# One share-split load per round, and a shorter VectorE chain per attention head, in a two-round cached decode kernel

## The chip, the cores and the metric

The kernel runs on one core of one Trainium2 chip. The metric is the device time of one execution in microseconds (us). Before the change it is 713.51 us, the median of three executions (712.98, 713.51, 714.87).

## What is computed

One token for each of 4 sequences goes twice through an attention layer and a two-matrix layer. Both rounds use the same weights and the same cache; of the cache only the last 1024 positions are read.

```
x = A_x                                        # (4, 1, 640)
for _ in range(2):
    q = layernorm(x) @ wq                      # 32 heads of 128
    scores = einsum("bhqd,bhkd->bhqk", q, k_cache[:, :, -1024:]) * 128 ** -0.5
    x = x + einsum("bhqk,bhkd->bhqd", softmax(scores), v_cache[:, :, -1024:]) @ wo
    x = x + maximum(layernorm(x) @ w1, 0) @ w2 # 640 -> 1728 -> 640
```

All numbers are float32. Each round reads every head's query weights, keys, values and output weights, and both matrices of the second layer, so about 302 MB cross from HBM to the core in one execution. The weights are read twice because the on-chip memory holds only a part of them.

## The kernel before

**Tiling.** The host lays everything that belongs to one head out as a *record*: 128 rows (partitions) of 9472 columns, in the order query weights (`WQ`, 640 columns), keys (`K`, 4096), values (`V`, 4096) and output weights (`WO`, 640). The tensor `rec` has the 32 records side by side. The tensor `wm` holds the two matrices of the second layer. On the chip the tile `store` has five slots of one record each; `ring`, `kept` and `kept2` hold further pieces.

**Loads.** A list `items` of pieces is made ahead, in the order in which they are needed; `piece`, `run` and `group` append to it. `pump` issues as many of them as have free room, from SyncE (SP). When an engine has used a piece, `done` marks its columns free and calls `pump` again, so a load's place in SP's program follows the work that frees its room, and SP waits there for that work. Before the change each load takes all 128 rows of a range of columns.

**Work of a head.** The loop over heads is written so that the work of neighbouring heads overlaps. TensorE (PE) runs its instructions in program order. For step n it computes the scores of head n+1 (`scores`, into one of two PSUM tiles `sc_ps`), the values product of head n (`values`, into `o_ps`), the query of head n+2 (`query`, into `misc`), and then the transposed output and the projection of head n (`output_T` into `o_ps`, `project` into `acc`). VectorE (DVE) finds the maximum of the scores, which ScalarE (ACT) needs for the exponentials (`softmax`); then VectorE transposes the exponentials in blocks of 32, scales them by one over their sum (`weights`) and picks the four diagonal blocks out of the values product (`picks`). The first records of round 2 are partly loaded while the second layer of round 1 runs. `park` and `unpark` hold some columns in PSUM meanwhile, and `mlp` is the second layer. `busy` issues matmuls whose results are not used.

**Lines.** Every instruction after the first few is recorded by the helper `InOrder`, so the profile gives nearly all of them line 104 (L104) and they are told apart by the names of their tiles: `sc_ps<-store,qT` are the scores, `o_ps<-store,scratch` the values product, `misc<-xT,store` the query, `o_ps<-pick,scratch` the transposed output, and `acc<-store,oTs` the projection. `acc<-store,scratch` is the last product of the second layer, and `store<-rec`, `ring<-wm` and `store<-wm` are loads. `t_ps<-sc_ps` is the transpose in `weights`, and `scratch<-o_ps,of_block` is `picks`.

## Time and profile before

| | |
|---|---|
| median of three executions | 713.51 us |
| the profiled execution's own time | 713.65 us |
| its span (first to last instruction) | 711.9 us |
| what lies around the span | 1.75 us |
| bytes read from HBM | 301.87 MB |
| PE, DVE, ACT busy | 498.0, 355.4, 95.9 us |
| mean granted TensorE clock | 0.83 |

The profile is of one execution. "Span" runs from the first to the last instruction. A row of a group names the engine, the operation, the tile written and the tiles read, the shape, how often it occurs, the busy time in us, the mean duration in ns, and after the second bar the idle time just before it with what ended that. A row by stretches of time gives, for each engine, the busy time and in brackets the number of instructions, then the granted clock, the mean busy share of the 16 DMA engines and the GB/s they moved. SPq is SP's queue of load issues.

### The profile page before, as it was taken

What the parts mean: (1) busy time and instruction counts of PE and PEld (TensorE: products, weight loads), DVE (VectorE), ACT (ScalarE), POOL (GpSimd) and SP (SyncE); (2) the same over time, 40 slices, a digit from 0 to 9 for tenths busy, and PEclk for the clock granted to TensorE, in tenths of its full rate; (3) what the DMA queues carried; (4) which work ended last, traced back from release to release, by engine and by line L of the source; (5) the groups of instructions that cost most, each with busy time, mean ns of one, the idle gap of its engine ahead of it and who ended that gap; (6) DMA issues with size and microseconds to landing.
All of it is one profiled execution on the core that took longest, in us unless ns stands there. A gap on an engine that the chain in (4) does not pass through costs nothing.

```text
span 711.9 us, 8953 instructions
## 1 busy us (share of the span) xinstructions
PE 498.0 (70%) x3718; PEld 200.7 (28%) x3718; DVE 355.4 (50%) x1008; ACT 95.9 (13%) x152; POOL 1.1 (0%) x9
## 2 busy tenths in 40 slices
PE   4387396476675576868878899666584578686976
PEld 2122132232321233333213343232231232233322
DVE  3254265253463354546741887644272454473761
ACT  1111010011010110111120321101010011020111
POOL 0000000000000000000000000000000000000000
PEclk9987678678787777788999999867697777788899
DMA  9999999999999999999999999999999999999996
GB/s 410 408 450 410 452 417 449 416 446 442 420 428 450 427 427 419 436 433 427 426 403 393 420 433 429 445 430 439 434 448 418 430 445 428 428 419 431 428 427 277
DMA packets 14760, 302.52 MB, mean 425 GB/s; under 512 B 1648, under 2 KB 2304, under 8 KB 6784
## 3 DMA queue, kind: packets, MB, share of 16 engines
q1 hardware_dynamic: 14688, 301.95, 99.0%
q8 instruction: 29, 0.48, 0.2%
q14 instruction: 11, 0.09, 0.0%
q10 hardware_dynamic: 32, 0.01, 0.0%
HBM read 301.87 MB, written 0.08 MB: 424 GB/s over the span
## 4 chain that ended last, share of the span: by engine, by line
DMA 75%; PE 20%; DVE 4%; issue 1%; ACT 0%; SPq 0%; DVEq 0%
DMA store<-rec 69%; PE o_ps L104 7%; PE sc_ps L104 6%; PE misc L104 4%; DMA ring<-wm 3%; DMA store<-wm 3%; PE acc L104 3%; DVE scratch L104 2%; DVE oTs L104 1%; DVE small L104 0%; ACT sc_ps L104 0%; PE t_ps L104 0%; SPq L104 0%; DVE store L104 0%; DVE t_ps L104 0%
## 5 line engine op out<-in xcount | busy, mean ns | idle before, releaser
L104 PE MATMUL sc_ps<-store,qT 128*4 128x512 f32 x1014 | 185.9, 827 | 33.4 <-DMA store<-rec 31.5
L104 PE MATMUL misc<-xT,store 128*128 128x4 f32 x640 | 99.0, 281 | 124.4 <-DMA store<-rec 124.0
L104 ACT ACTIVATE sc_ps<-sc_ps,small 128x1024 f32<-128x1024 f32 (+1 forms) x68 | 76.7, 1127 | 535.8 <-DVE small L104 535.3
L104 PEld LDWEIGHTS misc<-xT,store 128*128 128x128 f32 x640 | 93.4, 227 | 182.7 <-DMA store<-rec 150.9
L104 PE MATMUL o_ps<-store,scratch 128*16 128x512 f32 x956 | 140.3, 665 | 2.7 <-DVE scratch L104 1.5
L104 DVE TENSOR_REDUCE small<-sc_ps 128x1 f32<-128x1024 f32 x64 | 78.1, 1221 | 93.3 <-PE sc_ps L104 93.3
L104 DVE STREAM_TRANSPOSE t_ps<-sc_ps 128x512 f32<-128x512 f32 x128 | 93.1, 728 | 2.1
L104 DVE COPY qT<-misc 128x4 f32<-128x4 f32 x64 | 10.0, 156 | 142.8 <-PE misc L104 142.8
L104 DVE SCALAR_TENSOR_TENSOR scratch<-o_ps,of_block,scratch 128x128 f32<-128x128 f32 x186 | 65.2, 350 | 6.6
L104 PEld LDWEIGHTS sc_ps<-store,qT 128*4 128x4 f32 x1014 | 32.3, 106 | 113.6 <-issue 65.5
L104 PEld LDWEIGHTS o_ps<-store,scratch 128*16 128x16 f32 x956 | 32.1, 111 | 111.7 <-issue 67.6
L104 PE MATMUL acc<-store,oTs 128*4 128x160 f32 x478 | 33.4, 359 | 14.6 <-DVE oTs L104 13.2
L104 DVE TENSOR_SCALAR scratch<-o_ps,of_block 128x128 f32<-128x128 f32 x62 | 21.7, 350 | 30.4 <-PE o_ps L104 30.4
L104 PE MATMUL o_ps<-pick,scratch 128*128 128x4 f32 x124 | 26.6, 285 | 13.8 <-DVE scratch L104 13.8
L104 DVE TENSOR_TENSOR scratch<-t_ps,mrt 128x64 f32<-128x64 f32 x128 | 28.7, 225 | 4.7
L104 PEld LDWEIGHTS o_ps<-pick,scratch 128*128 128x128 f32 x124 | 22.5, 226 | 21.4 <-DVE scratch L104 18.8
L104 PE MATMUL misc<-store,small 128*1 128x512 f32 (+1 forms) x40 | 18.6, 570 | 1.7 <-DMA store<-rec 1.7
L104 DVE COPY oTs<-o_ps 128x4 f32<-128x4 f32 x58 | 9.4, 161 | 19.1 <-PE o_ps L104 18.6
L104 DVE TENSOR_SCALAR mrt<-of_batch,small 128x4 f32<-128x4 f32 x64 | 14.7, 230 | 2.2
L104 DVE STREAM_TRANSPOSE scratch<-small 128x32 f32<-128x32 f32 x64 | 12.9, 202 | 1.1 <-ACT sc_ps L104 1.1
L104 PEld LDWEIGHTS acc<-store,oTs 128*4 128x4 f32 x478 | 6.7, 84 | 20.6 <-DVE oTs L104 17.7
L104 ACT ACTIVATION_READ_ACCUMULATOR sc_ps<-sc_ps,small 128x1 f32 x64 | 12.2, 191 | 0.0
(76 smaller groups left out, 118.1 us busy)
## 6 DMA issues: line engine op xcount, KB each, us to landing
store<-rec SPq DMA_DIRECT2D x10, 7872.0 KB, 25.8
store<-rec SPq DMA_DIRECT2D x5, 7936.0 KB, 32.3
store<-rec SPq DMA_DIRECT2D x15, 2368.0 KB, 20.1
store<-rec SPq DMA_DIRECT2D x6, 4736.0 KB, 26.2
store<-rec SPq DMA_DIRECT2D x4, 6336.0 KB, 27.7
store<-rec SPq DMA_DIRECT2D x2, 7104.0 KB, 28.8
store<-rec SPq DMA_DIRECT2D x2, 6272.0 KB, 43.6
store<-rec SPq DMA_DIRECT2D x2, 4416.0 KB
```

What stands on the lines that cost most here:

```text
L104: r = build(*args, **kwargs)
```

## The change

Three things change.

1. **Loads.** In each round one record (head 25 in round 1, head 8 in round 2) gets its first 512 columns by a load of its own. The host stores these 512 columns a second time in a new tensor `shares` of 16 rows, 8 for each round. A row holds what 16 partitions of the tile take, one partition after the other (16 times 512 numbers), and 32 numbers of padding. The load's source is therefore 8 shares of 16 rows, where all other loads have 128 rows. The rest of the record comes as before, 8960 columns wide. The bytes moved are the same.
2. **VectorE.** `picks` is one product over 512 columns, written back into PSUM, and one sum over the four blocks, in the place of four instructions over 128 columns. `weights` transposes all 1024 columns in place and scales them in one instruction, in the place of two transposes into `t_ps` and two scalings.
3. **ScalarE.** It takes over four small operations per head: the copies to `qT` and to `oTs`, the product `nmax * rstd` in `softmax`, and `mrt` in `weights`. With the reading of the accumulated sum, which it did before, these are five small instructions beside the exponentials.

```
+SHARE = 512
+SHARED = [25, 8]
...
+    def shared(r, h):
+        src = shares[8 * r:8 * r + 8, :16 * SHARE].rearrange("g (p c) -> g p c", c=SHARE)
+        items.append((src, "store", home(h, r) * REC, SHARE, [(("rec", r, h), 0, SHARE, home(h, r) * REC)]))
+
     def piece(r, h, lo, hi, buf="store", col=None):
+        if h == SHARED[r]:
+            shared(r, h)
+            lo = SHARE
         run(r, h * REC + lo, h * REC + hi, buf, home(h, r) * REC + lo if col is None else col)
...
-        dve.tensor_copy(qT, misc[:, 8:8 + B])
+        act.copy(qT, misc[:, 8:8 + B])
...
-        dve.tensor_tensor(nmax, nmax, rstd, op=OP.mult)
+        act.activation(nmax, nmax, AF.Copy, scale=rstd)
         act.activation(sc_ps[s], sc_ps[s], AF.Exp, bias=nmax, scale=rstd, accum_out=tot[s])
 
-    def weights(s, parts=(0, 1)):
-        if 0 in parts:
+    def weights(s, parts=((0, 2),)):
+        if parts[0][0] == 0:
 
             dve.transpose(spread, tot[s].to_broadcast([P, 32]))
             dve.reciprocal(rtot, spread[:, 0:1])
-            dve.tensor_scalar(mrt, of_batch, rtot, None, op0=OP.mult)
-        for i in parts:
-            dve.transpose(t_ps, sc_ps[s][:, 512 * i:512 * i + 512])
-            dve.tensor_tensor(wT[:, i], t_ps.rearrange("p (c j) -> p c j", j=32)[:, :, :B],
-                              mrt.unsqueeze(1).to_broadcast([P, 16, B]), op=OP.mult)
+            act.activation(mrt, of_batch, AF.Copy, scale=rtot)
+        for i, j in parts:
+            w = sc_ps[s][:, 512 * i:512 * j]
+            dve.transpose(w, w)
+            dve.tensor_tensor(wT[:, i:j].rearrange("p i c j -> p (i c) j"),
+                              w.rearrange("p (c j) -> p c j", j=32)[:, :, :B],
+                              mrt.unsqueeze(1).to_broadcast([P, 16 * (j - i), B]), op=OP.mult)
...
     def picks(last):
-        o, on_ = outs[last], on[last]
-        dve.tensor_scalar(on_, o[:, :DH], of_block[:, 0:1], None, op0=OP.mult)
-        for c in range(1, 4):
-            dve.scalar_tensor_tensor(on_, o[:, DH * c:DH * c + DH], of_block[:, c:c + 1], on_, op0=OP.mult, op1=OP.add)
-
-    def output_T(i, last=False, by_act=False):
+        o = outs[last].rearrange("p (c d) -> p c d", c=4)
+        dve.tensor_tensor(o, o, of_block.unsqueeze(2).to_broadcast([P, 4, DH]), op=OP.mult)
+        dve.tensor_reduce(on[last], o.rearrange("p c d -> p d c"), op=OP.add, axis=AX.X)
+
+    def output_T(i, last=False):
         pe.matmul(outs[last][:, :B], on[last], pick, start=True, stop=True)
-        if by_act:
-            act.copy(oTs[:, i], outs[last][:, :B])
-        else:
-            dve.tensor_copy(oTs[:, i], outs[last][:, :B])
+        act.copy(oTs[:, i], outs[last][:, :B])
...
+        "shares": np.pad(np.concatenate([rec[h, :, :SHARE].reshape(8, 16 * SHARE) for h in SHARED]), ((0, 0), (0, 32))),
```

The last heads of a round keep two halves of 512 columns in `weights`, as before (`((0, 1),)`, `((1, 2),)` and `((0, 1), (1, 2))`). The added lines move the helper's line from 104 to 106.

The first place is SP, at the load of record 25 in round 1. `store<-rec 128x9472` is one whole record, and the wider loads ahead of it hold several records or parts of them. Before:

```order
L104 DMA store<-rec 128x15872
L104 DMA store<-rec 128x15744
L104 DMA store<-rec 128x9472
L104 DMA store<-rec 128x7296
L104 DMA kept<-rec 128x1536
```

With the change:

```order
L106 DMA store<-rec 128x15872
L106 DMA store<-rec 128x15744
L106 DMA store<-shares 128x1x512
L106 DMA store<-rec 128x8960
L106 DMA store<-rec 128x7296
L106 DMA kept<-rec 128x1536
```

The record's first 512 columns became a load of their own ahead of the rest; nothing else in SP's order moved.

The second place is VectorE, at the picks and weights of one early head in round 1, up to the next head's maximum (`sc_ps_74` and `sc_ps_75` are the two score tiles). Before:

```order
L104 TENSOR_SCALAR scratch<-o_ps,of_block 128x128
L104 SCALAR_TENSOR_TENSOR scratch<-o_ps,of_block,scratch 128x128 x3
L104 COPY qT<-misc 128x4
L104 COPY oTs<-o_ps 128x4
L104 STREAM_TRANSPOSE scratch<-small 128x32
L104 RECIPROCAL small<-scratch 128x1
L104 TENSOR_SCALAR mrt<-of_batch,small 128x4
L104 STREAM_TRANSPOSE t_ps<-sc_ps_75 128x512
L104 TENSOR_TENSOR scratch<-t_ps,mrt 128x64
L104 STREAM_TRANSPOSE t_ps<-sc_ps_75 128x512
L104 TENSOR_TENSOR scratch<-t_ps,mrt 128x64
L104 TENSOR_REDUCE small<-sc_ps_74 128x1
```

With the change:

```order
L106 TENSOR_TENSOR o_ps<-o_ps,of_block 128x512
L106 TENSOR_REDUCE scratch<-o_ps 128x128
L106 STREAM_TRANSPOSE scratch<-small 128x32
L106 RECIPROCAL small<-scratch 128x1
L106 STREAM_TRANSPOSE sc_ps_75<-sc_ps_75 128x1024
L106 TENSOR_TENSOR scratch<-sc_ps_75,mrt 128x128
L106 TENSOR_REDUCE small<-sc_ps_74 128x1
```

Fourteen instructions became seven; the fifteenth, the product `nmax * rstd` that follows the maximum, went as well.

The third place is ScalarE, in the early heads of round 1. Before, it has one instruction per head in this list (the reading of the sum belongs to it):

```order
L104 ACTIVATE sc_ps_74,small<-sc_ps_74,small 128x1024
L104 ACTIVATE sc_ps_75,small<-sc_ps_75,small 128x1024
L104 ACTIVATE sc_ps_74,small<-sc_ps_74,small 128x1024
L104 ACTIVATE sc_ps_75,small<-sc_ps_75,small 128x1024
L104 ACTIVATE sc_ps_74,small<-sc_ps_74,small 128x1024
```

With the change one head has:

```order
L106 COPY qT<-misc 128x4
L106 COPY oTs<-o_ps 128x4
L106 ACTIVATE mrt<-of_batch,small 128x4
L106 ACTIVATE small<-small 128x1
L106 ACTIVATE sc_ps_74,small<-sc_ps_74,small 128x1024
```

The two copies, `mrt` and the product for the maximum now stand between two exponentials in ScalarE's order.

More of the change, by code (lines that the diff above doesn't have):

```diff
@@ L111, in decode_kernel @@
 @with_exitstack
-def decode_kernel(ctx: ExitStack, tc: tile.TileContext, xf, rec, wm, out):
+def decode_kernel(ctx: ExitStack, tc: tile.TileContext, xf, rec, shares, wm, out):
     nc = tc.nc
@@ L517, in decode_kernel @@
                 scores(r, hs[-1], 1)
-                weights(s, (0,))
+                weights(s, ((0, 1),))
             if r and n < NS - 2:
                 busy(256, sc_ps[n % 2], 2, H - 1)
-            output_T(max(i, 0), by_act=end)
+            output_T(max(i, 0))
             if i < 0:
@@ L526, in decode_kernel @@
         softmax(1)
-        weights(0, (1,))
+        weights(0, ((1, 2),))
         values(r, hs[-2], 0, (0, 1))
-        weights(1)
+        weights(1, ((0, 1), (1, 2)))
         picks(0)
@@ L533, in decode_kernel @@
             park(0)
-        output_T(late - 2, by_act=True)
+        output_T(late - 2)
         if not r:
```

## Prediction

> **What bounds the kernel now.** I read the page's table of load queues first, then the chain of work that ended last, then the last microseconds in half-microsecond stretches. The page:
>
> ```profile
> span 711.9 us, 8953 instructions
> ...
> DMA packets 14760, 302.52 MB, mean 425 GB/s; under 512 B 1648, under 2 KB 2304, under 8 KB 6784
> ...
> q1 hardware_dynamic: 14688, 301.95, 99.0%
> q8 instruction: 29, 0.48, 0.2%
> q14 instruction: 11, 0.09, 0.0%
> q10 hardware_dynamic: 32, 0.01, 0.0%
> ...
> DMA 75%; PE 20%; DVE 4%; issue 1%; ACT 0%; SPq 0%; DVEq 0%
> ```
>
> The loads (q1) take 99.0% of what 16 DMA engines have in the span, and DMA holds 75% of the last chain. Two stretches show that this is so throughout, and two more show the change of rounds:
>
> ```profile
> 40.00:340.00 300.00, 203.21 (x1426) 82.78 (x1429) 147.74 (x414) 34.98 (x54) 0.00 (x0) 0.78 1.00 431
> ...
> 400.00:680.00 280.00, 204.93 (x1517) 83.39 (x1517) 155.29 (x437) 38.25 (x60) 0.00 (x0) 0.80 1.00 432
> ...
> 367.00:375.00 8.00, 5.77 (x43) 1.08 (x36) 0.48 (x3) 0.29 (x1) 0.00 (x0) 1.00 0.99 375
> 375.00:387.00 12.00, 10.44 (x137) 3.91 (x132) 0.87 (x2) 1.08 (x3) 0.00 (x0) 1.00 0.99 386
> ```
>
> In the 580 us of the first two rows the DMA share is 1.00, at 431 and 432 GB/s, while VectorE is busy about half the time. No VectorE time is saved there unless it lets a load start that otherwise would not; the engines have no free time in which it could run. What can still move the end is how evenly the 16 engines finish:
>
> ```profile
> 703.00:704.00 1.00, 1.00 (x36) 0.74 (x24) 0.00 (x0) 0.00 (x0) 0.00 (x0) 1.00 0.96 399
> 704.00:704.50 0.50, 0.25 (x4) 0.00 (x0) 0.00 (x0) 0.00 (x0) 0.00 (x0) 1.00 0.65 266
> 704.50:705.00 0.50, 0.00 (x0) 0.00 (x0) 0.00 (x0) 0.00 (x0) 0.00 (x0) 1.00 0.53 220
> 705.00:705.50 0.50, 0.00 (x0) 0.00 (x0) 0.00 (x0) 0.00 (x0) 0.00 (x0) 1.00 0.51 210
> 705.50:706.00 0.50, 0.00 (x0) 0.00 (x0) 0.00 (x0) 0.00 (x0) 0.00 (x0) 1.00 0.47 195
> 706.00:706.50 0.50, 0.35 (x12) 0.28 (x16) 0.00 (x0) 0.00 (x0) 0.00 (x0) 1.00 0.41 169
> 706.50:707.00 0.50, 0.50 (x24) 0.38 (x21) 0.00 (x0) 0.00 (x0) 0.00 (x0) 1.00 0.37 149
> 707.00:707.50 0.50, 0.50 (x23) 0.38 (x14) 0.00 (x0) 0.00 (x0) 0.00 (x0) 1.00 0.33 115
> 707.50:708.00 0.50, 0.50 (x22) 0.38 (x16) 0.00 (x0) 0.00 (x0) 0.00 (x0) 1.00 0.08 31
> ```
>
> The share does not fall at once. It falls to about one half by 704.5 (0.53 x 16 = 8.5 engines), stays near there and ends at about 707.5. So nearly half of the engines are through their last load 1 to 3.5 us ahead of the others. The capacity left idle is 0.5 x (0.35 + 0.47 + 0.49 + 0.53 + 0.59 + 0.63 + 0.67 + 0.92) = **2.33 us** of all 16 engines: the most that perfect levelling of this stretch could give. A likely cause, argued and not shown by these rows, is the fetching of instructions. The 29 packets of q8 took 0.2% of 16 x 711.9 us, or 22.8 engine-microseconds; on eight engines that is 2.85 us each, which is the size of the lateness. By their bytes they are TensorE's: 0.48 MB over the 7436 matmuls and weight loads is 65 B each.
>
> What follows the last load is fixed. The timeline of the end:
>
> ```profile
> 702.45 1.80 PE L104 MATMUL acc<-store,scratch 128*4 128x160 f32 x44 [0.83 <-DMA store<-wm]
> 706.15 2.00 PEld L104 LDWEIGHTS acc<-store,scratch 128*4 128x4 f32 x60 [2.25 <-DMA store<-wm]
> 706.15 2.76 PE L104 MATMUL acc<-store,scratch 128*4 128x160 f32 x68 [1.90 <-DMA store<-wm]
> ...
> 708.46 0.11 PEld L104 LDWEIGHTS acc<-store,scratch 128*4 128x4 f32 x8 [0.30 <-DMA store<-wm]
> 708.98 0.33 DVE L104 COPY scratch<-acc 128x160 f32<-128x160 f32 x1 [6.93 <-PE acc L104]
> 709.33 0.35 SPq L104 DMA_DIRECT2D out<-scratch  x1
> ```
>
> TensorE waits for three weight loads in a row (0.83, 1.90 and 0.30 us), and 711.9 - 708.46 = 3.4 us run from the last landing to the end. Loads that end earlier move the end by as much, up to the 1.90 us that TensorE has in hand at 706.15; beyond that its own work counts.
>
> **The shares.** 512 columns of 4 B in 8 rows are 16,384 B per engine when 16 engines carry them. One engine's rate is 432/16 = 27.0 GB/s, so that is 0.61 us. If eight shares go to eight engines, those carry 32,768 B and the other eight nothing: **+0.61 us** for the first, **-0.61 us** for the others, in each round. The bytes are the same. The 16 short rows of 2 KB may cost the eight engines a little: the stretch 375 to 387, full of rows of a few KB, ran at 386 instead of 432, which bounds the loss at 12% of 1.21 us, 0.15 us per round, below 0. I take nothing for it, because these engines are early.
>
> In round 2 this is worth 0.61 us at the end if the eight relieved engines are the late ones. Round 1's part must pass the change of rounds. There the loads are small and TensorE frees their room: at 375 and 386 GB/s against 432 the 20 us lose 8 x 0.13 + 12 x 0.11 = 2.4 us, partly because short rows are slower and partly because early engines stand idle until TensorE, which waits for the late ones, frees room. The late engines run through. So what they save in round 1 is kept, and what the early ones gain is taken from their idle time: 0.61 us more. Bounds for this part are 0 (the gate is TensorE's own work) and 0.61; I take 0.61, since at the end of the program, which is the same code with the same tiles, TensorE waits for the loads at every step (rows above). Sum: **-1.22 us**.
>
> Weighed beside it: the Trainium skill, "DMA: Bandwidth & Descriptors", section "Why a DMA increments its semaphore by 16 and not by 1", says that a load uses the largest number of engines up to 16 that divides the slowest dimension of both sides, and that these are the lowest-numbered ones. The packet counts agree on the number (14688 = 102 x (128 + 16) for 102 loads of 128 rows, and 32 = 4 x (4 + 4) for four loads of 4 rows, if each engine ends its part with one short packet), and by the rule 8 and 128 give eight engines. No row here shows which.
>
> **The engines' work per head.** The rows of before:
>
> ```profile
> L104 DVE TENSOR_REDUCE small<-sc_ps 128x1 f32<-128x1024 f32 x64 | 78.1, 1221 | 93.3 <-PE sc_ps L104 93.3
> L104 DVE STREAM_TRANSPOSE t_ps<-sc_ps 128x512 f32<-128x512 f32 x128 | 93.1, 728 | 2.1
> L104 DVE SCALAR_TENSOR_TENSOR scratch<-o_ps,of_block,scratch 128x128 f32<-128x128 f32 x186 | 65.2, 350 | 6.6
> L104 DVE TENSOR_SCALAR scratch<-o_ps,of_block 128x128 f32<-128x128 f32 x62 | 21.7, 350 | 30.4 <-PE o_ps L104 30.4
> L104 DVE TENSOR_TENSOR scratch<-t_ps,mrt 128x64 f32<-128x64 f32 x128 | 28.7, 225 | 4.7
> L104 DVE COPY oTs<-o_ps 128x4 f32<-128x4 f32 x58 | 9.4, 161 | 19.1 <-PE o_ps L104 18.6
> L104 DVE TENSOR_SCALAR mrt<-of_batch,small 128x4 f32<-128x4 f32 x64 | 14.7, 230 | 2.2
> L104 ACT ACTIVATE sc_ps<-sc_ps,small 128x1024 f32<-128x1024 f32 (+1 forms) x68 | 76.7, 1127 | 535.8 <-DVE small L104 535.3
> ```
>
> Picks were 4 x 0.350 = 1.40 us. The new product over 512 columns has no row; between a transpose of 512 (0.73) and four products of 128 (1.40) I take 0.73. The sum over 512 columns is half a maximum over 1024 and a little, 0.61 to 0.73; 0.7. Together 1.4: no change. Weights were 2 x 0.728 + 2 x 0.225 + 0.230 = 2.14. One transpose of 1024 lies between 1.22 (the maximum over 1024) and 1.46, one product of 128 between 0.225 and 0.45: about 1.65, so 0.5 less. The copies and small products, four of about 0.16 to 0.23, leave VectorE for ScalarE. VectorE loses some 1.0 us per head, about 65 us of its 355; ScalarE gains at most 4 x 0.26 (an estimate: its small operations cannot well exceed VectorE's 0.23 by much), some 65 us on 95.9. Neither becomes the bound. The first half of the weights comes later by 1.65 - (0.230 + 0.728 + 0.225) = 0.47 us, as TensorE used to begin on the first 512 columns; the second half comes earlier. Cover for all this is the queue of loads already issued, and this is how thick it is:
>
> ```profile
> SPq L104 <- PE acc L104: 385.5, 34, 27.0
> ...
> store<-rec SPq DMA_DIRECT2D x10, 7872.0 KB, 25.8
> ...
> 518.88 24.57 DMA store<-rec
> ...
> 619.57 24.86 DMA store<-rec
> ```
>
> SP waits 385.5 us for projections to free room, so a later projection does delay an issue. But in the chain the load issued at 518.88 is 24.57 us from issue to first use; 7872 KB at 432 GB/s take 18.7 us, and a lone load needs at most 711.9 - 709.33 = 2.6 us. That leaves about **3.3 us** in which earlier loads still kept the engines busy. A path that is 0.5 us longer costs nothing; one longer by over 3.3 us would cost the excess, at each of the thinnest places. I take 0.
>
> **Instruction fetches.** VectorE has some 8 x 64 = 512 instructions fewer and ScalarE 4 x 64 = 256 more. At 65 B that is 17 KB net, nothing. But q14's packets are of 8 KB (0.09 MB / 11), 0.3 us at 27.0 GB/s, and if one engine carries all of VectorE's it gets four fewer: -1.2 us for that engine, +0.6 for ScalarE's. For the end this is worth 0 unless that engine is last; I take 0 and keep -1.2 for the range.
>
> **Sum.** The profiled execution took 713.65 us (711.9 in the span and 1.75 around it), 0.14 above the median of 713.51. 713.65 - 1.22 = 712.43; from the median, 713.51 - 1.22 = **712.3 us**.
>
> **The rivals.**
> - *Levelling and fetch relief add up.* The late engine that ends last is the one with VectorE's fetches, and it gets 1.2 us besides: 713.51 - 1.22 - 1.2 = 711.1. For it: the whole idle stretch is 2.33 us, so there is room. Against: q14's bytes are a fifth of q8's. TensorE's 1.90 us in hand limit it too, unless its tail is shorter. 18%.
> - *The shares go to the busy half, or hold everybody up.* Then the late engines get 0.61 us more per round: 713.51 + 1.22 = 714.7. Nothing in the rows excludes it. The Trainium skill, "DMA: Bandwidth & Descriptors", "Rules for kernel authors", advises against a small outermost dimension, since it confines a load to that many engines; read as a cost, 1.21 us in the place of 0.61 per round gives that same +1.22. Against holding up: other loads are queued behind, at the cover worked out above. 11%.
> - *The loads run dry: slower.* ScalarE's copy to `oTs` now stands in its order behind an exponential of 1.13 us, and the projection that frees a slot waits for the copy. With the small product (0.26) that is at most 1.4 us per head; if three heads' work lies between a landing and the issue that it frees, 4.2 us, 0.9 over the 3.3 in hand. At four thin places per execution: +3.6, so 713.51 + 3.6 - 1.22 = 715.9 us; more, if more is late. It decides from 3.3 us of delay at one place. Against: the exponential has only to wait for the scores, ahead of the values and the next query in TensorE's order, so it is usually over. 8%.
> - *Nothing arrives.* TensorE's or VectorE's tail ends last, or the change of rounds gives the saving back: 713.5. 6%.
>
> **How the numbers follow.** The forecast has the remaining 57% and gives 712.3. A measurement of this kernel tells about 0.3%, 2.1 us, from no change: the forecast, the second rival and the fourth lie within it (74%), of which I give 2 points to a larger levelling. Faster by over 0.3% is the first rival with those two points, 20%; within 0.3% is 72%; slower is the third, 8%. The range runs from 710.8 (the first rival and 0.3 of spread between executions) to 714.1 (nothing arrives, and 0.6); it leaves out the second and third rival, 19%.
>
> **What would show it.** Right: the share of the DMA engines after 703 falls from near 1 to 0 within 1 to 2 us, not 3.5; TensorE's last waits for `store<-wm` are there still; the DMA share in the long stretches stays 1.00; VectorE is busy some 290 us and ScalarE some 160. Wrong: the half-empty stretch is as long or longer (the shares took the wrong half), or the share in a long stretch falls below 1.00 with SP waiting for `acc` (the third rival). A last wait that is for an engine, not a load, would be the fourth.

## The result, and the profile after

The changed kernel takes **718.16 us** (median of five executions, 717.32 to 718.84) against 713.51 before: 4.65 us more, ratio 1.006 with an interval of 1.0044 to 1.0076. The forecast was 712.3 with a range up to 714.1. It is slower by more than a measurement's uncertainty, and it lies above every rival's time.

The page of the changed kernel. The execution took 718.84 us, the longest of the five and 5.2 more than the profiled one of before; its span is 717.1:

```profile
span 717.1 us, 8757 instructions
PE 506.4 (71%) x3718; PEld 204.2 (28%) x3718; DVE 293.8 (41%) x508; ACT 148.8 (21%) x405; POOL 1.1 (0%) x9
...
DMA packets 15031, 302.51 MB, mean 422 GB/s; under 512 B 1664, under 2 KB 2320, under 8 KB 7056
...
q1 hardware_dynamic: 14960, 301.95, 98.7%
...
q14 instruction: 10, 0.08, 0.0%
...
DMA 75%; PE 20%; DVE 2%; ACT 1%; issue 1%; another core or an unknown queue 0%; SPq 0%
...
L106 DVE STREAM_TRANSPOSE sc_ps<-sc_ps 128x1024 f32<-128x1024 f32 (+1 forms) x68 | 80.5, 1183 | 0.1
...
L106 DVE TENSOR_TENSOR o_ps<-o_ps,of_block 128x512 f32<-128x512 f32 x62 | 43.3, 699 | 49.4 <-PE o_ps L106 49.4
...
L106 DVE TENSOR_REDUCE scratch<-o_ps 128x128 f32<-128x512 f32 x62 | 42.8, 691 | 2.1
...
L106 ACT ACTIVATE mrt<-of_batch,small 128x4 f32<-128x4 f32 x64 | 19.1, 299 | 1.4 <-DVE small L106 1.4
```

VectorE and ScalarE are busy 293.8 and 148.8 us, near the 290 and 160 that the prediction named, and the new operations cost what it took for them (0.699 and 0.691 us; 0.73 and 0.7 were taken). So the engines' work is as forecast, and the loads' share of the last chain is the same 75%. What fell is the rate: the loads moved the same 301.95 MB in 98.7% of a span that is 5 us longer. (Single executions of one kernel differ by a microsecond or two, so differences of that size between two traces are not the change's for certain.)

**Where the 5 us arise** can be read by following one instruction through both timelines. The scores of the second head of round 2 (16 matmuls), the first whose query's copy stands behind an exponential in the changed order, began at 394.15 before. The last large piece of the second layer (68 matmuls) began at 706.15. First before, then after:

```profile
393.85 0.16 DVE L104 COPY qT<-misc 128x4 f32<-128x4 f32 x1
...
394.15 1.90 PE L104 MATMUL sc_ps<-store,qT 128*4 128x512 f32 x16 [0.62 <-DVE qT L104]
```

```profile
390.70 2.10 PE L106 MATMUL sc_ps<-store,qT 128*4 128x512 f32 x8
...
393.25 1.45 PE L106 MATMUL sc_ps<-store,qT 128*4 128x512 f32 x8
...
396.48 1.18 ACT L106 ACTIVATE sc_ps<-sc_ps,small 128x1024 f32<-128x1024 f32 x1
...
397.58 0.19 ACT L106 ACTIVATION_READ_ACCUMULATOR sc_ps<-sc_ps,small 128x1 f32 x1
397.68 0.15 ACT L106 COPY qT<-misc 128x4 f32<-128x4 f32 x1
...
397.88 3.39 PE L106 MATMUL sc_ps<-store,qT 128*4 128x512 f32 x16 [1.98 <-ACT qT L106]
...
711.21 2.78 PE L106 MATMUL acc<-store,scratch 128*4 128x160 f32 x68 [1.83 <-DMA store<-wm]
```

At the change of rounds the program is 3.73 us late (397.88 - 394.15), at the end 5.06 (711.21 - 706.15). The timeline also shows a new wait, which is 1.36 us of the 3.73 (1.98 against 0.62). ScalarE's order has the query's copy behind the exponential (396.48 to 397.66) and the reading of its sum, so the copy that VectorE made at 393.85 comes last, TensorE waits 1.98 us for it, and the 16 matmuls take 3.39 us in the place of 1.90. The stretches around it, before and after:

```profile
396.00:398.00 2.00, 1.07 (x12) 0.13 (x8) 1.90 (x6) 0.00 (x0) 0.00 (x0) 1.00 1.13 443
398.00:400.00 2.00, 2.00 (x21) 1.14 (x18) 1.90 (x5) 0.61 (x1) 0.00 (x0) 1.00 1.00 419
```

```profile
392.00:394.00 2.00, 2.00 (x10) 0.61 (x10) 0.61 (x3) 0.78 (x2) 0.00 (x0) 0.50 1.01 392
...
396.00:398.00 2.00, 0.12 (x4) 0.11 (x8) 1.38 (x5) 1.64 (x4) 0.00 (x0) 0.88 0.90 308
398.00:400.00 2.00, 2.00 (x12) 0.30 (x8) 1.64 (x4) 0.30 (x1) 0.00 (x0) 0.50 0.30 116
400.00:410.00 10.00, 9.75 (x88) 3.96 (x80) 6.29 (x10) 3.28 (x8) 0.00 (x0) 0.95 0.93 372
```

TensorE idles from 396 to 398 (0.12 of 2 us busy), its granted clock is 0.50 in the next 2 us, and there the loads run dry: 116 GB/s at a DMA share of 0.30, where before they moved 419.

Not all of the 3.73 us follows from that wait. The first head's scores start at 390.70 and started at 390.01 before, so the program is only 0.69 us late there. Their two halves, eight matmuls each, take 2.10 and 1.45 us in the place of 1.03 and 1.04, at a granted clock that is 0.50 from 392 to 394, ahead of the wait. The clock falls there in the trace of e2 too (0.50 from 390 to 392), a kernel with the engine work of before, so this part isn't shown to come from the change.

The other loss is where the shares are loaded. The DMA view of 280 to 290 us, round 1's, gives packets, MB and the share of 16 engines' time, before and after:

```profile
q1 hardware_dynamic: 113, 3.98, 91.9%
```

```profile
q1 hardware_dynamic: 227, 3.25, 90.8%
```

The engines are about as busy as before (91 and 92%), but move 3.25 MB and not 3.98. The missing 0.73 MB is nearly three times what the share itself carries (128 x 2 KB = 0.26 MB): the engines do not wait, they are slow. The count of packets also tells how many engines carry a share: 14960 is 14688 + 2 x (128 + 8), so eight, if each engine ends its part with one packet, as the prediction read the count of before.

Round 2's share is loaded between 472 and 488 us. With the change, then in e2, which loads the same columns without a share:

```profile
q1 hardware_dynamic: 318, 6.35, 101.4%
```

```profile
q1 hardware_dynamic: 350, 7.05, 102.6%
```

Here too the engines are as busy and move 0.70 MB less.

The end of the loads, to be held against the half-microseconds that the prediction shows:

```profile
708.00:709.00 1.00, 1.00 (x36) 1.00 (x27) 0.17 (x1) 0.00 (x0) 0.00 (x0) 1.00 0.96 402
709.00:710.00 1.00, 0.38 (x8) 0.03 (x1) 0.00 (x0) 0.00 (x0) 0.00 (x0) 1.00 0.87 361
710.00:710.50 0.50, 0.00 (x0) 0.00 (x0) 0.00 (x0) 0.00 (x0) 0.00 (x0) 1.00 0.75 307
710.50:711.00 0.50, 0.00 (x0) 0.00 (x0) 0.00 (x0) 0.00 (x0) 0.00 (x0) 1.00 0.53 215
...
712.50:713.00 0.50, 0.50 (x20) 0.37 (x16) 0.00 (x0) 0.00 (x0) 0.00 (x0) 1.00 0.08 31
```

About half of the engines are through at 710.75 and the last at some 712.8, 2 us for what took 3 before. But from the first fall below 1 it takes 3.6 us (709 to 712.6), as long as before, and not the 1 to 2 us that the prediction named as its sign. What is left of this as levelling is said below, beside the end of e1.

### The profile page after: what moved, and what is told of

Same layout as the page of the kernel before. It is cut to its first block, busy times and chain, and to the rows that moved or that the text cites. A ratio compares the mean times of both kernels' runs of the same rounds, so it can differ in the third digit from the quotient of the medians.

```text
span 717.1 us, 8757 instructions
## 1 busy us (share of the span) xinstructions
PE 506.4 (71%) x3718; PEld 204.2 (28%) x3718; DVE 293.8 (41%) x508; ACT 148.8 (21%) x405; POOL 1.1 (0%) x9
## 3 DMA queue, kind: packets, MB, share of 16 engines
q1 hardware_dynamic: 14960, 301.95, 98.7%
## 4 chain that ended last, share of the span: by engine, by line
DMA 75%; PE 20%; DVE 2%; ACT 1%; issue 1%; another core or an unknown queue 0%; SPq 0%
DMA store<-rec 69%; PE sc_ps L106 7%; PE o_ps L106 6%; PE misc L106 4%; DMA ring<-wm 3%; DMA store<-wm 3%; PE acc L106 3%; DVE scratch L106 1%; DVE o_ps L106 1%; ACT oTs L106 1%; DVE small L106 0%; PE t_ps L106 0%; ACT sc_ps L106 0%; SPq L106 0%
## 5 line engine op out<-in xcount | busy, mean ns | idle before, releaser
L106 PE MATMUL sc_ps<-store,qT 128*4 128x512 f32 x1014 | 190.3, 841 | 40.2 <-DMA store<-rec 37.1
L106 PE MATMUL o_ps<-store,scratch 128*16 128x512 f32 x956 | 146.0, 686 | 2.1 <-DMA store<-rec 1.5
L106 ACT ACTIVATE small<-small 128x1 f32<-128x1 f32 x70 | 20.4, 292 | 313.4 <-DVE small L106 313.3
L106 DVE STREAM_TRANSPOSE sc_ps<-sc_ps 128x1024 f32<-128x1024 f32 (+1 forms) x68 | 80.5, 1183 | 0.1
L106 DVE TENSOR_TENSOR scratch<-sc_ps,mrt 128x128 f32<-128x128 f32 (+1 forms) x68 | 19.3, 284 | 122.0 <-ACT mrt L106 117.7
L106 DVE TENSOR_TENSOR o_ps<-o_ps,of_block 128x512 f32<-128x512 f32 x62 | 43.3, 699 | 49.4 <-PE o_ps L106 49.4
L106 ACT COPY qT<-misc 128x4 f32<-128x4 f32 x64 | 10.4, 162 | 176.6 <-PE misc L106 176.1
L106 DVE TENSOR_REDUCE scratch<-o_ps 128x128 f32<-128x512 f32 x62 | 42.8, 691 | 2.1
L106 ACT ACTIVATE mrt<-of_batch,small 128x4 f32<-128x4 f32 x64 | 19.1, 299 | 1.4 <-DVE small L106 1.4
L106 ACT COPY oTs<-o_ps 128x4 f32<-128x4 f32 x62 | 10.1, 162 | 33.7 <-PE o_ps L106 33.2
```

What stands on the lines that cost most here:

```text
L106: r = build(*args, **kwargs)
```

## The experiments

In all of them the kernel before ran on the same chip: 713.75, 713.38, 713.27 and 713.39 us in the four groups (e1 to e4, e5 to e8, e9 to e12, e13 to e16).

Two theories came from this reading: theory 1, that a share load slows all engines while it runs, and theory 2, that the copy of the query behind an exponential makes the loads run dry at the change of rounds. The rival of the first is the recorded forecast, by which the shares save 1.2 us; the rival of the second is that the engines' work costs nothing.

### Each half of the change alone

**e1, the loads alone.** The kernel before with part 1 of the change:

```
     def piece(r, h, lo, hi, buf="store", col=None):
+        if h == SHARED[r]:
+            shared(r, h)
+            lo = SHARE
```

> The kernel before with the two share loads alone; all engine work as before. In the profile with the change, the stretch from 280 to 286 us, in which the first share load runs, moved 317, 251 and 315 GB/s where the kernel before moved 315, 442 and 322 (a row's bytes count where its packets end, so the sum over the six us is what counts: 1766 against 2158 GB/us, 0.8 MB or 1.8 us less). Theory 1 (the share loads slow all engines while they run): about 1.8 us lost per share load, 3.6 for two, less what the levelling of the end gives back (0 to 1.2): +2.4 to +3.6 us, ratio 1.0035 to 1.005, and 280 to 286 as low as with the change. Theory 2 (the shares are harmless, the loss is in the change of rounds): the recorded forecast of the shares, -1.2 us, ratio 0.998, or at the least not slower than +0.3.

**718.45 us**, ratio 1.0065 (1.0053 to 1.0077). The shares alone cost as much as the whole change, 4.7 us, more than the 2.4 to 3.6 of theory 1, and the recorded forecast of a saving falls. The DMA view of 280 to 290 us:

```profile
q1 hardware_dynamic: 226, 3.27, 93.0%
```

And the two instructions followed above:

```profile
396.43 1.90 PE L106 MATMUL sc_ps<-store,qT 128*4 128x512 f32 x16 [0.62 <-DVE qT L106]
...
711.41 2.78 PE L106 MATMUL acc<-store,scratch 128*4 128x160 f32 x68 [1.93 <-DMA store<-wm]
```

2.28 us late at the change of rounds, 5.26 at the end: some 2.3 us in round 1 and 3.0 in round 2 of this execution (719.13 us), in the place of 0.61 saved in each. The end of e1's loads:

```profile
708.50:709.00 0.50, 0.50 (x24) 0.42 (x14) 0.00 (x0) 0.00 (x0) 0.00 (x0) 1.00 0.63 261
709.00:709.50 0.50, 0.48 (x12) 0.10 (x3) 0.00 (x0) 0.00 (x0) 0.00 (x0) 1.00 0.53 220
...
711.50:712.00 0.50, 0.50 (x20) 0.38 (x22) 0.00 (x0) 0.00 (x0) 0.00 (x0) 1.00 0.05 20
...
712.50:713.00 0.50, 0.50 (x22) 0.34 (x14) 0.00 (x0) 0.00 (x0) 0.00 (x0) 1.00 0.18 58
```

From 0.53 the share is down at 0.05 after 2.5 us, but the last loads land only at some 713.4, over 4 us after it, against some 3 before and 2 after the change.

**e2, the split without shares.** The same 512 columns as a load of their own, of 128 rows from `rec`:

```
+        if h == SHARED[r] and lo == 0:
+            run(r, h * REC, h * REC + SHARE, buf, home(h, r) * REC)
+            lo = SHARE
```

> The kernel before, with the same 512 columns of the same two records loaded by a load of their own, but of all 128 rows and from the record itself, so that 16 engines carry it as before. It has the short rows and the added load of the share loads without the eight-engine split. Theory 1: no loss, since each engine keeps its own rows: within 0.3 us of before, ratio 1.000, and no dip in the GB/s where it runs. Rival (a load of its own with rows of 2 KB is itself what slows): the loss of the share loads, +1 to +3.6 us.

**714.01 us**, 1.0008 (0.9998 to 1.0019): no difference that can be told. The same stretch:

```profile
q1 hardware_dynamic: 257, 4.06, 94.8%
```

One more load and its short pieces cost nothing to speak of: 4.06 MB in 94.8% is 26.8 GB/s per busy engine (4.06 / (0.948 x 160 us)), as before (3.98 / (0.919 x 160) = 27.1). In e1 it is 3.27 / (0.930 x 160) = 22.0. This rate is the measure in what follows.

**e3, the engines' work alone.** The changed kernel without part 1:

```
     def piece(r, h, lo, hi, buf="store", col=None):
-        if h == SHARED[r]:
-            shared(r, h)
-            lo = SHARE
```

> The changed kernel with its VectorE and ScalarE code, without the share loads. In the profile with the change, 398 to 400 us has a DMA share of 0.30 and 400 to 410 one of 0.93, together about 2.1 us without loads, where the kernel before has 1.00 and 1.02; TensorE stood idle for 1.98 us there, waiting for ScalarE's copy to qT, which is behind the exponential in ScalarE's order. Theory 2 (the change of rounds runs dry because of that copy and because TensorE's granted clock falls to 0.5 after the idle time): +2 to +3 us, ratio 1.003 to 1.004, and a DMA share clearly below 1 between 395 and 410. Theory 1 alone (all is in the share loads): within 0.5 us of before. The recorded forecast for the engine work: 0.

**714.48 us**, 1.0012 (1.0001 to 1.0023): 0.7 over before, less than the 2 to 3 of theory 2 and a little more than the 0.5 of theory 1. The wait, the slow matmuls and the fall of the rate at the change of rounds are here too:

```profile
395.09 3.42 PE L104 MATMUL sc_ps<-store,qT 128*4 128x512 f32 x16 [1.97 <-ACT qT L104]
```

```profile
396.00:398.00 2.00, 2.00 (x12) 0.36 (x8) 0.88 (x2) 0.00 (x0) 0.00 (x0) 0.50 0.91 266
398.00:400.00 2.00, 2.00 (x20) 0.42 (x12) 1.23 (x1) 0.18 (x1) 0.00 (x0) 0.81 0.76 280
```

**e4, the same with the query's copy back on VectorE.**

```
-        act.copy(qT, misc[:, 8:8 + B])
+        dve.tensor_copy(qT, misc[:, 8:8 + B])
```

> As the run before it, with one line put back: the copy to qT is VectorE's again, in all heads. All the rest of the new VectorE and ScalarE code stays. Theory 2: the first scores of round 2's second head no longer wait for the exponential, TensorE's idle time of 1.98 us there goes, the DMA share between 395 and 410 is back near 1.00, and the time is within 0.5 us of before (ratio 0.9995 to 1.0005), some 2 to 3 us below the run without this line. Rival (the loss in the change of rounds comes from the other new instructions, or from where TensorE's clock happens to fall): the time stays where the run before it was.

**712.71 us**, 0.9983 (0.9975 to 0.9992): the one version here that beats the kernel before by more than the spread, where theory 2 had it within 0.5 us of before. The dip is gone:

```profile
396.00:398.00 2.00, 1.15 (x12) 0.37 (x16) 1.82 (x3) 0.04 (x1) 0.00 (x0) 1.00 1.12 460
398.00:400.00 2.00, 2.00 (x20) 1.28 (x14) 1.14 (x2) 1.55 (x3) 0.00 (x0) 1.00 0.98 418
```

So moving one copy of 0.15 us to ScalarE costs 1.8 us, and the rest of the engines' work saves about 1.

### Is it one place, and where does the saving come from?

**e7, VectorE copies the query of one head per round only,** the second, whose copy stands behind the first exponential.

```
-        query(r, hs[1])
+        query(r, hs[1], True)
```

> The change without its shares, with the copy to qT put back on VectorE for one head per round only: the second head of the round, whose query is computed ahead of the first exponential of the round. Earlier runs: all of the engine work without shares 714.48; the same with every copy to qT back on VectorE 712.71. Theory P (one place): the whole difference of 1.8 us comes from the change of rounds, where the copy stands behind the first exponential, TensorE is idle for 2 us and its granted clock falls to 0.50; then 712.7 +-0.5, and the stretch 396 to 398 moves over 400 GB/s. Theory H (each head): the copies of all heads add a little to every head's path; then 714.1 to 714.5.

**713.05 us**, 0.9993 (0.9984 to 1.0002), within theory P and outside theory H. By the medians alone, one copy per round brings back 1.4 of the 1.8 us. But e7 ran in another group than e3 and e4. When each is held against the kernel before of its own group, e3 is 0.73 us slower, e7 0.33 faster and e4 1.04 faster, so it brings back 1.1 of the 1.8. The scores follow VectorE's copy at once:

```profile
393.61 0.14 DVE L104 COPY qT<-misc 128x4 f32<-128x4 f32 x1
...
393.90 1.90 PE L104 MATMUL sc_ps<-store,qT 128*4 128x512 f32 x16 [0.41 <-DVE qT L104]
```

The other 62 copies on ScalarE may hold the 0.3 to 0.7 us that are left; the intervals of e7 and e4 overlap, so this is not told from nothing. Most of the loss is at one place; whether all of it is stays open.

**e8, e4 with short instructions added** where VectorE has time:

```
             if not end:
                 weights(s)
+                if 5 <= n < 27:
+                    for _ in range(10):
+                        dve.memset(unused, 0.0)
```

> The change without shares and with every copy to qT on VectorE (712.71 earlier), plus ten short memsets on VectorE per head in heads 5 to 26 of each round, 440 in all, after the weights of the head. VectorE has 1099 instructions then, 659 without them and 1033 before the change; it is busy about half of the time and these stretches have a DMA share of 1.00, so its own time has room. Theory F (fetches): e4 is faster than before because VectorE's instructions are fetched through the same DMA engines, and fewer of them make one engine less late; then the memsets take the gain away, 713.4 to 713.9. Theory C (chain): the gain comes from shorter chains of VectorE at the changes of rounds and at the end, where no memset stands; then it stays, 712.4 to 713.0.

**714.54 us**, 1.0021 (1.0013 to 1.0029), 1.8 us over e4 (2.2 when each is held against the kernel before beside it), more than the whole saving and above the range of theory F. VectorE has about as many instructions as before the change (1012 and 1008 in the profiles), ScalarE has more (340 and 152). The groups and queues of e8, then the queue of e4:

```profile
q14 instruction: 13, 0.11, 0.0%
...
L104 DVE MEMSET small<- 128x1 f32 (+1 forms) x443 | 26.1, 59 | 26.5
```

```profile
q14 instruction: 9, 0.07, 0.0%
```

The memsets are 26.1 us of work on an engine that is busy less than half of the time, in stretches at a DMA share of 1.00; as work on VectorE they are hidden. What grows with them is q14, from 9 packets to 13. With 9, 11 and 13 packets the times are 712.71, 713.4 (before) and 714.54: about 0.45 us for each. Theory F holds in direction. It is shown that more short instructions cost time here although VectorE has room for them; that it is the packets which do it rests on this row of three. A rival that no run tests is that ten memsets per head, 0.6 us, make VectorE's chain longer, and with it the projection that frees room for a load.

### Why a share load is slow

**e5, sixteen shares of 8 rows.**

```
-        src = shares[8 * r:8 * r + 8, :16 * SHARE].rearrange("g (p c) -> g p c", c=SHARE)
+        src = shares[16 * r:16 * r + 16, :8 * SHARE].rearrange("g (p c) -> g p c", c=SHARE)
```

> Before, with the same 512 columns of one record per round as sixteen shares of 8 rows in the place of eight of 16; nothing else is changed. Earlier run: the eight shares alone gave 718.45 us, 4.7 over before (713.75), and the stretches from 280 to 286 us moved 348, 301 and 287 GB/s where the plain split into two loads moved 319, 352 and 501. Theory A (too few engines): the loss comes from eight engines that carry all of the load while the other eight are ahead or behind; sixteen engines share it evenly, so 714.0 (like the plain split), +-0.5, with no dip after the load. Theory B (the rows): the loss comes from which partitions an engine writes, because with a block of neighbouring partitions it writes where other engines write at the same time; sixteen shares of 8 neighbouring rows still do that, so 716 to 719 and a dip below 350 GB/s over some 6 us after the load. A result between 714.5 and 716 leaves both a part.

**716.29 us**, 1.0048 (1.0036 to 1.006). The stretch 280 to 290:

```profile
q1 hardware_dynamic: 241, 3.52, 93.5%
```

Sixteen engines carry it (two loads of 128 + 16 packets), and still it costs 2.9 us and runs at 23.5 GB/s per busy engine. Theory A, eight engines in the place of sixteen, expected 714.0 and is not the main cause, though sixteen engines lose 1.8 us less than the eight of e1; theory B, the partitions written, holds its range.

**e6, four loads of 32 rows, each of eight shares of 4 rows.**

```
+        src = [shares[32 * r + 8 * j:32 * r + 8 * j + 8, :4 * SHARE].rearrange("g (p c) -> g p c", c=SHARE)
+               for j in range(4)]
```

> Before, with the same 512 columns as four loads of 32 rows, each as eight shares of 4 rows; again eight engines carry all the bytes if eight shares go to eight engines, 32 KB each, but each engine writes four neighbouring partitions at a time in each of the four quarters, not sixteen in one block. Theory A (too few engines): as the eight shares of 16 rows, 717.5 to 719. Theory B (the rows): less of the loss, 713 to 716; if the four-row pattern takes all of it away, the recorded forecast's gain of 0.6 per round could show, 712.5 to 713.5. SP issues three more loads per round, which these rows price at nothing while others are queued.

**717.27 us**, 1.0054 (1.0042 to 1.0066), between what the two theories gave: this run does not decide.

**e9, e10, e11, the place of the rows in HBM.** The rows of `shares` are first 36 KB apart, then as far apart as those of `rec`; last, a small tensor is read by a usual load of 128 rows.

```
-... for h in SHARED]), ((0, 0), (0, 32))),
+... for h in SHARED]), ((0, 0), (0, 1024))),
```

```
+... for h in SHARED]), ((0, 0), (0, H * REC - 16 * SHARE))),
```

```
+        src = shares[P * r:P * r + P, :SHARE]
```

> The shares alone (718.45 earlier), with one number changed: the padding of a row of the share tensor is 4096 B and not 128 B, so the eight rows that eight engines read at once lie 36 KB apart and not 32 KB and 128 B. What is written, by whom and in which order stays the same. Theory S (source): the loss comes from where the rows lie in HBM, since eight streams with almost the same pitch as a power of two get in each other's way, and everybody else's too; then the loss is gone, 712.3 to 714.5, and no stretch from 280 to 290 us moves less than the plain split there. Theory B (the rows written) and theory A (eight engines): nothing changes, 718 to 719.

> The shares alone, with the rows of the share tensor as far apart as those of the records, 1,212,416 B. Theory S (source), in the form that the rows' pitch decides or that 256 KB in one place of HBM are too little to be read by eight engines at once: the loss is gone, 712.3 to 714.5; and if the recorded forecast is right about the late engines, its 0.6 us per round appears only now, 712.3 to 713. Theories A and B: 718 to 719, as before. If the padding of 4 KB leaves the loss and this one takes it away, it is the place (one small stretch of HBM), not the pitch.

> The plain split (714.01 earlier), with its 128 rows of 512 columns read from a small tensor of their own (rows 2176 B apart, 272 KB per round in one stretch), by the usual load of 128 rows; the partitions that an engine writes are as for any other load. Theory S, form place (one small stretch of HBM): the loss of the shares is here too, 716 to 719. Theory S, form pitch, and theories A and B: as the plain split, 713.5 to 714.5.

**718.01, 718.37 and 713.46 us**; ratios 1.006 (1.0047 to 1.0072), 1.0065 (1.0053 to 1.0077) and 1.0 (0.9991 to 1.0009). The stretch 280 to 290 of e10 and of e11:

```profile
q1 hardware_dynamic: 224, 3.14, 89.9%
```

```profile
q1 hardware_dynamic: 256, 4.03, 93.9%
```

21.8 GB/s per busy engine with the rows far apart (22.0 in e1, where they are close), 26.8 from the small tensor read by 128 rows. Theory S is out in both forms. The Trainium skill, "DMA: Bandwidth & Descriptors", "Latency and other measured facts", has copies between HBM tensors slowed by row pitches at large powers of two, from 512 KiB on, and restored at 4 MiB by 4 KiB more. The loads here have pitches of 32,896, 36,864 and 1,212,416 B, none of them such a power, and differ by less than the spread: the pitch is not what costs here, and the page's own case is not tested.

**e12, the whole change with far rows and the query's copy on VectorE.**

```
-        act.copy(qT, misc[:, 8:8 + B])
+        dve.tensor_copy(qT, misc[:, 8:8 + B])
...
+... for h in SHARED]), ((0, 0), (0, H * REC - 16 * SHARE))),
```

> The whole change with two edits: the copy to qT back on VectorE, and the rows of the share tensor 1,212,416 B apart. If theory S holds and the recorded forecast was right about the late engines, the two add up: 712.71 (engine work with qT on VectorE, earlier) less up to 1.2, 711.5 to 712.7. If S holds and the levelling is worth nothing: 712.7 to 713.3. If S falls: 717 or more.

**716.43 us**, 1.0042 (1.0028 to 1.0057). With the copy back the time is 1.7 us below the change's 718.16 (1.5 when each is held against the kernel before beside it), as it was 1.8 below e3's; if that is the copy's doing, the far rows bring nothing, as theory S falling would have it, though less is lost than the 717 that was expected then.

**e13, two plain loads of 64 rows** from `rec`, no shares:

```
+            items.append((
+                [(p, rec[p, h * REC:h * REC + SHARE]) for p in (slice(0, 64), slice(64, P))],
```

> The plain split (714.01 earlier), with the 512 columns as two plain loads of 64 rows from the records themselves in the place of one of 128. No share tensor; sixteen engines if the rule of 64 rows holds. Theory W (the partitions written): a load of another number of rows than 128 puts rows on other engines than the loads before and behind it, so two engines write to the same part of the memory; then a loss of a part of the shares' size, 714.8 to 717, and a dip at 282 to 286 us. Theory D (the form of the shares, 16 short pieces out of one long row, is slow by itself): as the plain split, 713.5 to 714.4.

**716.29 us**, 1.0036 (1.0023 to 1.0049), and in 280 to 290:

```profile
q1 hardware_dynamic: 257, 3.49, 92.6%
```

23.6 GB/s. A plain load of 64 rows does it too; the packets (15008 = 14688 + 4 x (64 + 16)) say that sixteen engines carry it. The special form of a share is not needed for the loss. What e2 and e11 have, and none of the kernels slowed in this way has, is that every large load is of 128 rows.

**e14 and e15, twins:** two loads of 32 rows by shares and a plain load of 64, the shares on partitions 0 to 63 or on 64 to 127.

```
+        src = [(slice(32 * j, 32 * j + 32),
+                shares[32 * r + 8 * j:32 * r + 8 * j + 8, :4 * SHARE].rearrange("g (p c) -> g p c", c=SHARE))
+               for j in (0, 1)]
+        src.append((slice(64, P), rec[slice(64, P), h * REC:h * REC + SHARE]))
```

```
+               for j in (2, 3)]
+        src.append((slice(0, 64), rec[slice(0, 64), h * REC:h * REC + SHARE]))
```

> Before, with the 512 columns as three loads: partitions 0 to 31 and 32 to 63 by eight shares of 4 rows each, partitions 64 to 127 by a plain load of 64 rows. Theory W, with the mapping that the Trainium skill gives (below): share e of these two loads goes where engine e writes in any load of 128 rows, so only the plain load is off; well below its twin (e15), by 0.8 us or more. Theory D: the twin's time within 0.5 us. The Trainium skill, DMA: Bandwidth & Descriptors, The descriptor swizzle, gives for 128 partitions engines 0 to 7 to partitions 0 to 63, four neighbouring ones at a time and again 32 further on, and engines 8 to 15 to the rest in the same way.

> The twin of the one before: partitions 64 to 95 and 96 to 127 by eight shares of 4 rows each, partitions 0 to 63 by a plain load of 64 rows. The numbers of loads, engines, bytes and pieces are the same. Theory W: all of the shares' bytes are written where other engines (8 to 15) write, so the loss is 0.8 us or more above the twin's, 715.5 to 718. Theory D: the twin's time within 0.5 us.

**716.33 and 718.00 us**, 1.0039 (1.0027 to 1.0051) and 1.0064 (1.0052 to 1.0076). The stretch 280 to 290, low, then high:

```profile
q1 hardware_dynamic: 261, 3.63, 93.3%
```

```profile
q1 hardware_dynamic: 255, 3.42, 93.9%
```

The same number of loads, engines, pieces and bytes differ by 1.7 us (24.3 and 22.8 GB/s) for nothing but which partitions are written by which load. Theory W called the side and the least distance; theory D falls. By the Trainium skill, "DMA: Bandwidth & Descriptors", "The descriptor swizzle", named in the expectation, the low twin's share engines write where they also write in loads of 128 rows, and the high twin's do not, if eight shares go to engines 0 to 7 in order. The runs agree in the side; no view shows the engines.

The sizes do not follow from theory W. In e14 only the plain load of 64 rows should be off, yet e14 loses 2.9 us, as much as e13 with two such loads. In e6 half of the shares lie where they lie in e14, yet e6 loses 3.9 us, more than e5 with its sixteen shares (2.9). The twins also swap the half that the plain load writes, and no run has the shares of one half without it.

**e16, 256 columns per share load.**

```
-SHARE = 512
+SHARE = 256
```

> The shares alone (718.45), with 256 columns in the place of 512: half of the bytes, pieces of 1 KB. If the loss goes with the bytes written (theory W, or A): about half, 715.3 to 716.5. If it is fixed per load (an event at its start or end, or the same number of 128 pieces): 717.5 to 718.7.

**715.81 us** median, but the interval of the ratio is 1.0031 to 1.0084, because three executions took 720 to 724 us. The median is what a loss that goes with the bytes gives (2.4 us, half of 4.7). The trace, of an execution of 717.02 us, does not show half: from 260 to 320 us the loads moved 25.06 MB, as in e1, where before they moved 25.91. Whether the loss goes with the bytes stays open.

## Why the prediction was wrong, step by step

**The shares, forecast -1.22, measured +4.7.** The step that failed is the cost of the share load itself: "I take nothing for it, because these engines are early", with a bound of 0.15 us per round from the stretch 375 to 387. That stretch has short rows, but they come in loads of 128 rows, like all big loads of the kernel before; a load of another shape had no row, and the bound was none. It costs some 2.3 us per load, and not by its own bytes alone: the sixteen engines together are as busy as before and move a fifth less while it is loaded. What the runs put in its place is that a small load beside the stream costs this when it is not of 128 rows (e13 against e2), and that which partitions it writes changes the cost (e14 against e15). That it does so by writing partitions from other engines than the loads around it, so that two engines share one way into the memory, as the Trainium skill's section on the descriptor swizzle suggests, is argued: no view here names the engine of a packet, and the sizes in e6 and e14 do not follow from it. The second rival had "hold everybody up" in words, but only at the price of the share's own bytes. Round 1's half of the term had a second weak step: it took the early engines to be idle for part of 367 to 387 us, but the two rows shown for it have a DMA share of 0.99, which leaves at most 0.2 us of idle time in those 20.

**The levelling** (0.61 us in each round) stays open. The half-empty stretch at the end takes 3 us before and 2 after the change, but that does not point the forecast's way. Summed as the prediction sums it, over the eight half-microseconds up to the last landing, the capacity left idle is 2.33 us before and 1.82 after the change; with shares it is 3.08 in e1, 2.97 in e9 and 2.71 in e10, and without them 3.16 in e2, 2.06 in e11 and 1.62 in e4. Kernels with shares do not lie lower as a group, and the ends of single executions differ by more than the 0.61 us that was sought. No kernel here has shares without the loss, so what the levelling would be worth isn't shown.

**The engines' work, forecast 0.** The durations were right, and in the long stretches nothing of it shows, as forecast. The step that failed is "a path that is 0.5 us longer costs nothing", for which 3.3 us of cover had been worked out from loads of whole records in the middle of a round. At the change of rounds the cover is thinner, and the path is not 0.47 but 2.9 us longer there: 1.36 of waiting (1.98 - 0.62) and 1.49 of slower matmuls (3.39 - 1.90). The slow matmuls alone need not make the loads run dry: in e5's trace the same 16 matmuls took 3.49 us, after a wait of 0.62 us, and the DMA share from 396 to 400 was 1.06 and 1.03. The third rival named this very mechanism, ScalarE's order, but for the copy to `oTs` and at four thin places; the copies to `qT` did it, at 1.8 us, of which one copy per round, the second head's, makes 1.1 to 1.4.

**Instruction fetches, forecast 0 with -1.2 kept for the range.** e4 gains 1.0 us and e8 loses it again. The value kept for the range was about the right one. That fewer instructions are worth time although VectorE has room for them is shown; that the fetches are the reason, as the first rival has it, is not, and the match in size may be luck.

**The sum** of the three is 4.7 + 1.8 - 1.0 = 5.5 against 4.65 measured. Where the parts overlap by 0.85 isn't resolved; and these are single groups of executions, whose medians differ by some tenths for the same kernel (713.27 to 713.75 before).

## What to carry to other kernels

In a kernel that is bound by its loads, try to send them all in one shape: here a small load that was not of 128 rows cost two to four times what its own bytes take (1.4 to 2.3 us per round against 0.61). Before a small operation moves to a less busy engine, read what stands ahead of it in that engine's order at the thinnest place of the program, not in the middle of a round. And a bound is only as good as its row: where no row shows an operation, the range has to say so.

## What the hardware showed beyond that

- In both traces with a TensorE wait of some 2 us at the change of rounds (the change, 1.98; e3, 1.97) the matmuls behind it ran at a granted clock of 0.50 and took 3.39 and 3.42 us in the place of 1.90. In e5 they took 3.49 after a wait of only 0.62, so the long wait is not needed for it.
- 440 memsets of 59 ns, on an engine that is busy less than half of the time, cost 1.8 us.
- Two loads of 64 rows in the place of one of 128, beside loads of 128 rows, lowered the mean rate of a busy DMA engine from 26.8 to 23.6 GB/s over 10 us.
